# Strassen weight blocks made with single copies and single differences, and size sums added up in FP32

## The chip, the cores and the metric

One core of one Trainium2 chip runs the kernel in one launch. The metric is the device time in microseconds, from the start to the end of the launch. The engines are PE (TensorE), DVE (VectorE), ACT (ScalarE), POOL (GpSimd) and SP (SyncE, which here only issues DMAs). Each works through its own queue in order, and they wait for each other on semaphores.

## The reference

Two kinds of layer alternate, A, B, A, B, over 2048 tokens of width 1024; each adds its result to x, and both use the same weights in either round.

```
A: h = layernorm(x);  q, k, v = h @ wqkv          (32 heads of 32)
   each token attends to 8 positions: itself and 2, 4, .. 14 back
   x = x + (softmax(q.k / sqrt(32)) . v) @ wo
B: h = layernorm(x)
   x = x + (silu(h @ w1) * (h @ w3)) @ w2          (hidden width 3584)
```

## The kernel before

**Stages.** Tokens go in chunks of 512. The first A layer's q, k and v come first (to about 190 us). Then come eight units, each a B layer of one chunk: units 0 to 3 for the first round, 4 to 7 for the second. In units 1 to 4 the q, k and v of the second A layer's chunks are made behind the B layer. Attention is VectorE work: products of q and shifted k (L597), folded by a tree of additions (L510, L512, L514), a gather on PE into the PSUM tile `L` (L611), softmax, and the same tree for v (L682). The result oT goes through wo on PE (`po`, L788) and is added to x (L793). The hidden width is done in two splits, of 16 and 12 blocks of 128.

**Plain units and Strassen units.** Units 0 and 1 (`u < TU`) use plain products: `pg` (L1307) and `pu` (L1316) for w1 and w3, and `acc` (L1338) for w2. From unit 2 on (`pipeline`, `products`, tile `st`, L1074, and `w`, L1193) a product of 2 x 2 quarters is made with seven products P1 to P7 instead of eight. For that the weights are needed in FP16 as seven blocks: the four quarters and three sums and differences of them. Units 0 and 1 make these blocks beside their own work and store them to DRAM (`t_d` for w1 and w3, `t2_d` for w2); later units load them as `early`, `late` and `t2`.

**Making the blocks.** This is what the change touches. For each of 14 weight tiles (7 column groups of w1 and of w3):

- ACT squares the tile and sums it by rows (`weight_size`, L895). PE adds the 128 rows up with a product by a tile of ones (`size`, L909), DVE reduces that (L901) and makes a power of two of it (L883 to L887), `up_scale`, so that the FP16 blocks keep in range. For w2 as a whole `total_scale` does the same once (L1016).
- ACT copies the quarters, scaled, into a block buffer (`weight_sums`, L927); DVE makes the other three (`diff_steps`, L939 to L941); POOL stores the seven (L949, L950). A tile has two such blocks of columns, `a` = 0 and 1, and there are two block buffers, both in the tile `big`. A buffer is written again when its store has landed.
- For w2 (`sums_of_w2`) 14 blocks are made in the same way, with the copies at L1032 and the store at L1040.

That makes 28 blocks of w1 and w3, and 14 of w2. The two buffers, and the two PSUM banks of the pool `side`, from which `size`, `po` and `L` all take their tiles, are shared. Six other PSUM banks serve all wide products.

**Weights.** All weight tiles, the Strassen blocks too, rotate through six buffers (`wp`) in the order of the list `seq`, loaded by SP. In units 0 and 1 a buffer of w1 or w3 is given back only when its blocks are made (`release_held`), one of w2 likewise (`finish_sums`). SP issues in program order, so a load that waits holds up all that stands behind it, the DMA transposes of the normalised x (`xnT`, L272) among them, as these hold up loads.

**What sets the order.** The order of every queue is fixed when the program is built, by a planner that keeps an expected time for each engine (`now`). Each background step is yielded with its expected cost and the time from which it is ready:

```
yield 1.20, max(got["at"], stored[a]), lambda: nc.scalar.activation(...)
```

For ACT `act_background` emits steps as long as the step ends before `now["pe"] + gate[0]`, that is 2.2 us past PE's expected time. For DVE `background` takes, among the queues of makes, norms, adds, values and scores, the step that can start first and ends in time. A load, a `po` tile or a release is emitted when the planner sees its input done. So a step of another cost moves other steps too. In Strassen units the exponential of the scores (L639) is not emitted at once but put into `later` and issued by `run_later` (L1097), behind the copy of the third product of a group (P6).

Of the kernel before, what the change touches and what calls it, by code (L numbers as in the profile page):

```python
# [7 lines left out]
FP32 = mybir.dt.float32  # L8
BF16 = mybir.dt.bfloat16
FP16 = mybir.dt.float16  # L10
I32 = mybir.dt.int32
ALU = mybir.AluOpType
ACTF = mybir.ActivationFunctionType
# [4 lines left out]
def kernel(  # L18
# [13 lines left out]
    nc = tc.nc  # L32
    cfg = dict(cfg or {})
    P = 128
    _, S, D = A_x.shape
    F = B_w1.shape[1]
    KT = D // P
    W, DIL, Dh = 8, 2, 32
    assert D == 1024 and KT == 8 and D // Dh == 32
    CH = 512  # L40
# [15 lines left out]
    fsplits = [(0, 16), (16, NF)] if NF > 16 else [(0, NF)]  # L56
# [11 lines left out]
    const = ctx.enter_context(tc.tile_pool(name="const", bufs=1))  # L68
# [135 lines left out]
    HT = TCH  # L204
    big = const.tile([P, 7168], FP16, name="big")
    sums = big[:, 0:3072].rearrange("p (s k t) -> p s k t", s=3, k=KT // 2)
# [2 lines left out]
    tight = big[:, 6144:7168].bitcast(BF16).rearrange("p (i a t) -> p i a t", i=2, a=2)  # L209
    blocks = [big[:, 3584 * i:3584 * (i + 1)].rearrange("p (b k c) -> p b k c", b=7, k=KT // 2) for i in range(2)]  # L210
    NG = NF // FG
    ones = const.tile([P, P], BF16, name="ones")
    nc.gpsimd.memset(ones[:], 1.0)
    size = const.tile([P, 2, NG, 2], FP32, name="size")
    up_scale = const.tile([P, 2, NG], FP32, name="up_scale")
# [69 lines left out]
    def norm_sums(key):  # L285
# [5 lines left out]
        for name, i, out, x, y, op in (("P5", 0, s1, a21, a22, ALU.add), ("P6", 1, s2, s1, a11, ALU.subtract),  # L291
                                       ("P3", 2, s4, a12, s2, ALU.subtract), ("P7", 3, a21, a11, a21, ALU.subtract)):
            while (sums_free[i] is None) if i < 3 else key in plain_left:
# [401 lines left out]
    seq = [("qkv", which, h) for which in range(3) for h in range(2)]  # L695
    for u in range(len(units)):
        for f0, f1 in fsplits:
            if u >= TU:
                groups = [(m, g0 // FG) for g0 in range(f0, f1, FG) for m in range(2)]
                for i, (m, g) in enumerate(groups):  # L700
                    seq += [("early", m, g)] + ([("late", *groups[i - 1])] if i else [])
                seq += [("late", *groups[-1])]
            for g0 in range(f0, f1, FG) if u < TU else ():
                seq += [(kind, g0, min(FG, f1 - g0), (u, g0 // FG) if m == u else None)
                        for m, kind in enumerate(("w1", "w3"))]
            nq = (f1 - f0) // 2
            if u >= TU:
                seq += [("t2", fsplits.index((f0, f1)), b, nq) for b in (0, 2, 1, 3, 4, 6, 5)]
            else:
                seq += [("w2", g0, nq, hh) for hh in range(2) for g0 in (f0, f0 + nq)]  # L710
        if 1 <= u and u + 3 < len(units):
            seq += [("qkv", which, h) for which in range(3) for h in range(2)]
# [176 lines left out]
    def weight_size(m, g, w, at, got):  # L889

        w_ = w[:].rearrange("p k c -> p (k c)")
        half = w_.shape[1] // 2
        up, down = up_scale[:, m, g:g + 1], down_scale[:, m, g:g + 1]
        for i in range(2):
            yield 1.95, at, lambda: nc.scalar.activation(junk, w_[:, i * half:(i + 1) * half], ACTF.Square,  # L895
                                                         accum_out=size[:, m, g, i:i + 1])

        def scale_item(ps, r):
            def emit():
                opened[0] -= 1  # L900
                nc.vector.tensor_reduce(down, ps[:], op=ALU.add, axis=AX.X)  # L901
                scale_of(down, up, down)
                got["at"] = now["dve"] + 0.1
            yield 1.0, r, emit

        def add_up(t):
            ps = side_tile([P, 2], FP32, name="size", tag="sd")
            opened[0] += 1
            nc.tensor.matmul(ps[:], lhsT=ones[:], rhs=size[:, m, g, :].bitcast(BF16)[:, 1::2], start=True, stop=True)  # L909
            makes.insert(0, [scale_item(ps, pe(1, t)), None])  # L910

        t = now["act"] + 2.5
        pe_queue.append((lambda: t, lambda: add_up(t)))

    def weight_sums(m, g, w, got):

        while "at" not in got:
            yield "blocked"
        KQ = KT // 2
        for a in range(2):  # L920
            while pending[a]:
                yield "blocked"
            pending[a] += 1
            b = blocks[a]
            for i, j, fh in ((0, 2, 0), (3, 6, 1)):
                c0 = fh * 256 + a * P
                yield 1.20, max(got["at"], stored[a]), lambda: nc.scalar.activation(  # L927
                    b[:, i:j + 1:j - i], w[:, :, c0:c0 + P].rearrange("p (h k) c -> p h k c", h=2), ACTF.Copy,
                    scale=up_scale[:, m, g:g + 1])
            makes.append([differences(m, g, a, now["act"] + 0.1), None])  # L930
        made.add((m, g))

    pending, stored, made, held = [0] * 2, [0.0] * 2, set(), []
    junk = hsum[:].bitcast(BF16).rearrange("p k t -> p (k t)")

    def diff_steps(b):

        tt = nc.vector.tensor_tensor
        yield 0.66, lambda: tt(b[:, 1:5:3], b[:, 3:7:3], b[:, 0:4:3], op=ALU.subtract)  # L939
        yield 0.42, lambda: tt(b[:, 3], b[:, 4], b[:, 0], op=ALU.add)  # L940
        yield 0.42, lambda: tt(b[:, 5], b[:, 2], b[:, 3], op=ALU.subtract)  # L941

    def differences(m, g, a, r):

        b = blocks[a]
        for step in diff_steps(b):
            yield step[0], r, step[1]
        pending[a] -= 1
        nc.gpsimd.dma_start(t_d[m][g][:, 4 * a:4 * (a + 1)], b[:, 0:4])  # L949
        nc.gpsimd.dma_start(t_d[m][g][:, 8 + 3 * a:8 + 3 * (a + 1)], b[:, 4:7])  # L950
        stored[a] = now["dve"] + 7.0
# [49 lines left out]
    def total_scale(sizes_, up, down, got):  # L1001

        n = sizes_.shape[1]

        def scale_item(ps, r):
            def emit():
                opened[0] -= 1
                nc.vector.tensor_reduce(total[:], ps[:], op=ALU.add, axis=AX.X)
                scale_of(total[:], up[:], down[:])
                got["at"] = now["dve"] + 0.1  # L1010
            yield 1.1, r, emit

        def add_up(t):
            ps = side_tile([P, n], FP32, name="size", tag="sd")
            opened[0] += 1
            nc.tensor.matmul(ps[:], lhsT=ones[:], rhs=sizes_[:].bitcast(BF16)[:, 1::2], start=True, stop=True)  # L1016
            makes.insert(0, [scale_item(ps, pe(1, t)), None])

        t = now["act"] + 2.5
        pe_queue.append((lambda: t, lambda: add_up(t)))  # L1020
# [3 lines left out]
    def sums_of_w2(i, f, ws, loaded):  # L1024

        while "at" not in got2 or all(pending):
            yield "blocked"
        a = min((i for i in range(2) if not pending[i]), key=lambda i: stored[i])
        pending[a] += 1
        b = big[:, a * 3584:(a + 1) * 3584].rearrange("p (b c) -> p b c", b=7)  # L1030
        for j, (fh, hh) in ((0, (0, 0)), (3, (0, 1)), (2, (1, 0)), (6, (1, 1))):
            yield 0.61, max(loaded, stored[a], got2["at"]), lambda: nc.scalar.activation(b[:, j], ws[hh][fh][:, f, :], ACTF.Copy,  # L1032
                                                                             scale=up2[:])
        r = now["act"] + 0.1

        def rest():
            for step in diff_steps(b):
                yield step[0], r, step[1]
            pending[a] -= 1
            nc.gpsimd.dma_start(t2_d[i][:, :, f, :], b)  # L1040
            stored[a] = now["dve"] + 7.0

        makes.append([rest(), None])
        made.add(("w2", i, f))
# [12 lines left out]
    def pipeline(key, groups, consume, done, last, fill=None):  # L1057

        xnT = xnTs[key]
        KQ = KT // 2  # L1060
        sides = dict(P1=(0, xnT[:, 0:KQ, 0:HT]), P5=(1, sums[:, 0]), P6=(3, sums[:, 1]), P2=(2, xnT[:, KQ:KT, 0:HT]),
                     P7=(0, xnT[:, 0:KQ, HT:CH]), P3=(2, sums[:, 2]), P4=(1, xnT[:, KQ:KT, HT:CH]))

        def acc():
            return psum.tile([P, 2, HT], FP32, name="st", tag="mm")
# [1 line left out]
        def run(G, name, out, start, ready=0.0):  # L1067
            if name in ("P5", "P6", "P7", "P3"):
                force(adds, lambda: (key, name) in sums_at)
# [8 lines left out]
        def head_part(i, name):  # L1078
# [22 lines left out]
            elif name == "P2":  # L1101
                r = run(G, name, G["B"], False, G["tB"])
                release(1)
                consume(G, 0, G["B"][:], r)
            elif name == "P7":
                G["late"] = weight("late")
# [19 lines left out]
        for i in range(n + 1):  # L1126
            if i == n:
                staged[0] = False
                while later:
                    later.pop(0)[1]()  # L1130
            for name, tail in (("P1", "P7"), ("P5", "P3"), ("P6", "P4"), ("P2", None)):
                if i < n:
# [15 lines left out]
    def products(u, f0, f1, hold):  # L1148
# [8 lines left out]
        H11, H12, H21, H22 = [h16[:, k0:k0 + nq, t0:t0 + HT] for t0 in (0, HT) for k0 in (0, nq)]  # L1157
        left = dict(P1=H11, P2=H12, P5=hsum, P6=H11, P7=H21, P3=H12, P4=H22)
        H, ready_at, pieces, w2 = [{}, {}], {}, [0], {}
# [281 lines left out]
```

## Time and the profile before

| | |
|---|---|
| median of 3 runs | 1553.25 us (1551.62 to 1554.37) |
| profiled execution: time | 1551.62 us |
| its span, first to last instruction | 1549.7 us |
| PE, DVE, ACT, POOL busy | 1525.7, 1198.2, 874.1, 162.5 us |
| mean granted TensorE clock | 0.997 |
| size products (L909, L1016) | 15, from 194.5 to 484.1 us |
| copies of w1 and w3 quarters (L927) | 56 of 128x1024, 61.8 us busy |
| copies of w2 quarters (L1032) | 56 of 128x512, 35.5 us busy |
| differences (L939, L940, L941) | 42 each, 28.8, 17.7, 17.8 us busy |

Times in views are microseconds from the start of the span. A row of the timeline gives start, length, engine, line, operation, output and inputs, and in brackets the idle time of the engine before it and what ended that. A row of the groups gives one line's instructions of one shape: how many, their busy time in all, the mean of one in ns, and the idle time before them with its causes. A PE product overlaps the next one, so its own length (379 ns for 512 columns) is more than its share of the stream. SPq rows show the time for which SP was busy issuing.

### The profile page before, as it was taken

The numbers are of one execution on the slowest core, as the hardware profiler recorded it, in microseconds if no ns is written. First come the engines' busy times: TensorE is split into PE (matmuls) and PEld (weight loads), VectorE is DVE, ScalarE is ACT, GpSimd is POOL, SyncE is SP. The second block draws the span as 40 slices with busy tenths as digits, with TensorE's granted clock in tenths as the row PEclk, the third lists the DMA queues.
The fourth block names the chain that finished last, engine by engine and source line by source line (L and its number), as shares of the span: only waits on it lengthen the run. The fifth ranks groups of instructions, "written<-read, shape, count | busy, mean of one in ns | idle before, by whom it ended". The sixth has DMA issues, their size and how long they took to land.

```text
span 1549.7 us, 24962 instructions
## 1 busy us (share of the span) xinstructions
PE 1525.7 (98%) x9619; PEld 986.9 (64%) x9619; DVE 1198.2 (77%) x2084; ACT 874.1 (56%) x1332; POOL 162.5 (10%) x308
## 2 busy tenths in 40 slices
PE   9999999999999899999999999999999999999999
PEld 7666644444444467675685857767677667686866
DVE  4788999789869787979898967798768977445345
ACT  4885465556456246655565654655658356554634
POOL 1210111121211100102101020010102001000000
PEclk9999999999999999999999999999999999999999
DMA  9876969798687997988979888798979988878885
GB/s 331 200 225 203 275 206 298 266 319 297 215 309 268 252 322 257 332 287 298 294 257 326 317 291 282 268 325 288 325 264 310 333 305 285 295 274 339 310 294 206
DMA packets 261431, 439.55 MB, mean 284 GB/s; under 512 B 73856, under 2 KB 201088, under 8 KB 245056
## 3 DMA queue, kind: packets, MB, share of 16 engines
q1 hardware_dynamic: 248464, 390.90, 76.2%
q0 software_dynamic: 12704, 46.93, 8.4%
q8 instruction: 75, 1.23, 0.3%
q14 instruction: 44, 0.36, 0.1%
q10 hardware_dynamic: 144, 0.13, 0.0%
HBM read 345.90 MB, written 67.90 MB: 267 GB/s over the span
## 4 chain that ended last, share of the span: by engine, by line
PE 53%; DVE 11%; DMA 5%; ACT 4%; issue 2%; POOL 0%; ACTq 0%; DVEq 0%; SPq 0%; POOLq 0%
PE st L1074 27%; PE w L1193 15%; PE ps L853 7%; PE po L788 5%; DMA t_d<-big 3%; DVE tree L682 2%; DVE tree L510 2%; DVE tree L597 1%; DMA xnT<-xn 1%; DMA w3t<-in_B_w_dram 1%; DVE tree L512 1%; ACT sg L1255 1%; DMA kT<-qkv_d 1%; DVE hT L1320 1%; DVE big L939 1%
## 5 line engine op out<-in xcount | busy, mean ns | idle before, releaser
L853 PE MATMUL ps<-xnT,wqkv 128*128 128x512 f16 (+1 forms) x1472 | 322.3, 381 | 5.2 <-DMA wqkv<-in_A_wqkv_dram 3.8
L1074 PEld LDWEIGHTS <-early 128*128 128x128 f16 x2688 | 262.6, 98 | 40.7 <-issue 3.7
L853 PEld LDWEIGHTS <-wqkv 128*128 128x128 bf16 x1472 | 210.6, 144 | 115.2 <-DMA wqkv<-in_A_wqkv_dram 6.2
L1193 PE MATMUL w<-t,hT 128*128 128x512 f16 x1008 | 225.9, 379 | 1.2 <-ACT big L1213 1.1
L1074 PEld LDWEIGHTS <-late 128*128 128x128 f16 x2016 | 197.1, 98 | 31.9 <-issue 4.2
L597 DVE TENSOR_TENSOR tree<-qT,kT 128x2048 bf16<-128x2048 bf16 x128 | 156.2, 1220 | 31.2 <-ACT big L857 15.0
L510 DVE TENSOR_TENSOR tree<-tree 128x1024 bf16<-128x1024 bf16 x256 | 174.8, 683 | 0.9
L1074 PE MATMUL st<-xnT,late 128*128 128x256 f16 x1344 | 174.2, 273 | 0.7 <-DVE big L1111 0.2
L1074 PE MATMUL st<-big,early 128*128 128x256 f16 x1344 | 172.2, 273 | 1.9 <-ACT st L1086 1.8
L1193 PEld LDWEIGHTS <-hT 128*128 128x128 f16 x1008 | 98.3, 98 | 113.7 <-issue 2.4
L1074 PE MATMUL st<-xnT,early 128*128 128x256 f16 x1344 | 166.0, 273 | 0.0
L682 DVE TENSOR_TENSOR tree<-At,vT 128x2048 bf16<-128x2048 bf16 x128 | 156.0, 1219 | 11.0 <-DMA At<-E 9.6
L788 PE MATMUL po<-wo,oT 128*128 128x512 bf16 x512 | 117.7, 382 | 5.2 <-DVE down_scale L901 4.4
L1086 ACT COPY st<-st 128x512 f32<-128x512 f32 x84 | 48.4, 577 | 129.9 <-PE st L1074 129.3
L1316 PE MATMUL pu<-xnT,w3t 128*128 128x512 f16 x448 | 107.2, 383 | 2.8 <-DMA w3t<-in_B_w_dram 2.8
L857 ACT CAST hT<-ps 128x512 bf16<-128x512 f32 x96 | 55.5, 586 | 90.1 <-PE ps L853 89.0
L1307 PE MATMUL pg<-xnT,w1t 128*128 128x512 f16 x448 | 106.1, 380 | 0.0
L1338 PE MATMUL acc<-w2t,hT 128*128 128x512 bf16 x448 | 98.0, 379 | 0.2 <-DVE hT L1320 0.2
L1099 DVE TENSOR_TENSOR st<-st,big 128x512 f32<-128x512 f32 x84 | 58.4, 695 | 50.7 <-ACT big L1095 50.5
L1255 ACT ACTIVATE sg<-st,down_scale 128x512 bf16<-128x512 f32 x126 | 86.7, 688 | 12.7 <-PE st L1074 12.3
L788 PEld LDWEIGHTS <-oT 128*128 128x128 bf16 x512 | 50.1, 98 | 62.4 <-issue 8.3
L1074 PE MATMUL st<-big,late 128*128 128x256 f16 x672 | 87.1, 273 | 1.8 <-DVE st L1099 1.8
(168 smaller groups left out, 1903.1 us busy)
## 6 DMA issues: line engine op xcount, KB each, us to landing
early<-t_d SPq DMA_DIRECT2D x84, 1024.0 KB, 6.1
late<-t_d SPq DMA_DIRECT2D x84, 768.0 KB, 6.5
t<-t_d SPq DMA_DIRECT2D x42, 1024.0 KB, 7.2
t<-t_d SPq DMA_DIRECT2D x42, 768.0 KB, 5.3
wqkv<-in_A_wqkv_dram SPq DMA_DIRECT2D x28, 1024.0 KB, 7.4
w1t<-in_B_w_dram SPq DMA_DIRECT2D x14, 1024.0 KB, 8.4
w3t<-in_B_w_dram SPq DMA_DIRECT2D x14, 1024.0 KB, 11.4
t_d<-big POOLq DMA_DIRECT2D x28, 512.0 KB, 6.5
```

What stands on the lines that cost most here:

```text
L510: nc.vector.tensor_tensor(b, b, buf[:, 4:8, :], op=ALU.add)
L597: V.tensor_tensor(pr, qT[:], kT[:, :, k0:k0 + TCH], op=ALU.mult)
L682: V.tensor_tensor(tm.rearrange("p w (a e) -> p w a e", a=4), At[:].rearrange("p a w e -> p w a e"), win, op=ALU.mult)
L788: nc.tensor.matmul(ps[:], lhsT=oT[:, t, j * P:(j + 1) * P], rhs=wo[:, t, hh * 512:(hh + 1) * 512], start=(t == 0), stop=(t == KT - 1))
L853: nc.tensor.matmul(ps[:], lhsT=ws[kk // KH][:, kk % KH, t::KT], rhs=xnT[:, kk, :], start=(kk == 0), stop=(kk == KT - 1))
L1074: nc.tensor.matmul(out[:, a, :], lhsT=w[:, a, blk, k, :], rhs=rhs[:, k, :], start=start and a == 0 and k == 0, stop=k == KQ - 1, skip_grou ...
L1099: nc.vector.tensor_tensor(G["D"][:], G["D"][:], su, op=ALU.add)
L1193: nc.tensor.matmul(out[:], lhsT=lhs[:, k, j * P:(j + 1) * P], rhs=w[:, k, :], start=start and k == 0, stop=k == nq - 1, skip_group_check=True)
L1255: nc.scalar.activation(sg[:], src, ACTF.Silu, scale=inv)
L1307: nc.tensor.matmul(pg[:], lhsT=w1t[:, kk, fi * P:(fi + 1) * P], rhs=xnT[:, kk, :], start=(kk == 0), stop=(kk == KT - 1))
L1316: nc.tensor.matmul(pu[:], lhsT=w3t[:, kk, fi * P:(fi + 1) * P], rhs=xnT[:, kk, :], start=(kk == 0), stop=(kk == KT - 1))
L1338: nc.tensor.matmul(acc[:], lhsT=hT[:, f, j * P:(j + 1) * P], rhs=tiles[hh][f // nq][:, f % nq, :], start=(f == 0), stop=(f == f1 - f0 - 1))
```

## The change

The change came with the name "in Strassen units the exponential of the scores is issued on ScalarE right behind the copy of a group's third product, not as soon as its input is ready". The diff does not touch that place: `later`, `run_later` and the line that calls it stand in both programs. It does this:

- The tile of ones becomes FP32, and the size products take the FP32 sums whole, where before they took the upper 16 bits of each as BF16.
- For w1 and w3 each block's quarters are copied one by one (four ACT copies of 128x512, planned at 0.61 us) and not in pairs (two of 128x1024, planned at 1.20).
- The three derived blocks are made with four differences of 128x512 (planned at 0.40 us each) and not with one of 128x1024 and two of 128x512 (0.66, 0.42, 0.42), for w1 and w3 and for w2.
- The blocks stand at other places of the seven, and the tables that name them (`sides`, the t2 entries of `seq`) follow.

```
-    ones = const.tile([P, P], BF16, name="ones")
+    ones = const.tile([P, P], FP32, name="ones")
...
-                seq += [("t2", fsplits.index((f0, f1)), b, nq) for b in (0, 2, 1, 3, 4, 6, 5)]
+                seq += [("t2", fsplits.index((f0, f1)), b, nq) for b in range(7)]
...
-            nc.tensor.matmul(ps[:], lhsT=ones[:], rhs=size[:, m, g, :].bitcast(BF16)[:, 1::2], start=True, stop=True)
+            nc.tensor.matmul(ps[:], lhsT=ones[:], rhs=size[:, m, g, :], start=True, stop=True)
...
-            for i, j, fh in ((0, 2, 0), (3, 6, 1)):
+            for i, (kh, fh) in ((0, (0, 0)), (1, (0, 1)), (3, (1, 0)), (5, (1, 1))):
                 c0 = fh * 256 + a * P
-                yield 1.20, max(got["at"], stored[a]), lambda: nc.scalar.activation(
-                    b[:, i:j + 1:j - i], w[:, :, c0:c0 + P].rearrange("p (h k) c -> p h k c", h=2), ACTF.Copy,
+                yield 0.61, max(got["at"], stored[a]), lambda: nc.scalar.activation(
+                    b[:, i], w[:, kh * KQ:(kh + 1) * KQ, c0:c0 + P], ACTF.Copy,
                     scale=up_scale[:, m, g:g + 1])
...
-    def diff_steps(b):
-
-        tt = nc.vector.tensor_tensor
-        yield 0.66, lambda: tt(b[:, 1:5:3], b[:, 3:7:3], b[:, 0:4:3], op=ALU.subtract)
-        yield 0.42, lambda: tt(b[:, 3], b[:, 4], b[:, 0], op=ALU.add)
-        yield 0.42, lambda: tt(b[:, 5], b[:, 2], b[:, 3], op=ALU.subtract)
-
     def differences(m, g, a, r):
 
         b = blocks[a]
-        for step in diff_steps(b):
-            yield step[0], r, step[1]
+        for out, x, y in ((4, 5, 1), (1, 1, 0), (2, 4, 0), (6, 3, 2)):
+            yield 0.40, r, lambda: nc.vector.tensor_tensor(
+                b[:, out], b[:, x], b[:, y], op=ALU.add if (x, y) == (4, 0) else ALU.subtract)
...
-            nc.tensor.matmul(ps[:], lhsT=ones[:], rhs=sizes_[:].bitcast(BF16)[:, 1::2], start=True, stop=True)
+            nc.tensor.matmul(ps[:], lhsT=ones[:], rhs=sizes_[:], start=True, stop=True)
...
-        for j, (fh, hh) in ((0, (0, 0)), (3, (0, 1)), (2, (1, 0)), (6, (1, 1))):
+        for j, (fh, hh) in ((0, (0, 0)), (2, (0, 1)), (1, (1, 0)), (5, (1, 1))):
...
-            for step in diff_steps(b):
-                yield step[0], r, step[1]
+            for out, x, y in ((4, 5, 2), (2, 2, 0), (3, 4, 0), (6, 1, 3)):
+                yield 0.40, r, lambda: nc.vector.tensor_tensor(
+                b[:, out], b[:, x], b[:, y], op=ALU.add if (x, y) == (4, 0) else ALU.subtract)
...
-        sides = dict(P1=(0, xnT[:, 0:KQ, 0:HT]), P5=(1, sums[:, 0]), P6=(3, sums[:, 1]), P2=(2, xnT[:, KQ:KT, 0:HT]),
-                     P7=(0, xnT[:, 0:KQ, HT:CH]), P3=(2, sums[:, 2]), P4=(1, xnT[:, KQ:KT, HT:CH]))
+        sides = dict(P1=(0, xnT[:, 0:KQ, 0:HT]), P5=(1, sums[:, 0]), P6=(2, sums[:, 1]), P2=(3, xnT[:, KQ:KT, 0:HT]),
+                     P7=(0, xnT[:, 0:KQ, HT:CH]), P3=(1, sums[:, 2]), P4=(2, xnT[:, KQ:KT, HT:CH]))
```

## The prediction

> **What bounds the kernel now.** I read the page's first part first, then the busy times of four stretches.
>
> ```profile
> span 1549.7 us, 24962 instructions
> PE 1525.7 (98%) x9619; PEld 986.9 (64%) x9619; DVE 1198.2 (77%) x2084; ACT 874.1 (56%) x1332; POOL 162.5 (10%) x308
> ```
>
> ```profile
> 0.00:194.00 194.00, 192.51 (x1105) 126.49 (x1106) 148.74 (x244) 118.99 (x196) 26.74 (x62) 1.00 0.84 247
> 194.00:524.00 330.00, 321.46 (x1500) 143.74 (x1497) 285.80 (x560) 189.44 (x233) 57.55 (x94) 0.99 0.82 269
> 524.00:620.00 96.00, 88.82 (x576) 63.62 (x577) 68.38 (x114) 44.12 (x71) 4.36 (x8) 0.98 0.89 287
> 620.00:1550.00 930.00, 922.94 (x6443) 653.09 (x6440) 695.26 (x1168) 521.60 (x834) 73.90 (x144) 1.00 0.86 296
> ```
>
> The columns after the length are PE, PEld, DVE, ACT and POOL busy, then granted clock, DMA share and GB/s. PE bounds every stretch. The edited work all lies from 194 to 524 us (the size products run from 194.5 to 484.1 us), and just there and behind it PE loses time: 8.5 and 7.2 us idle, at a granted clock of 0.99 and 0.98. Past 620 us it idles 7 us in 930, so what is won or lost before reaches the end. Where PE stands still, its timeline says (start, length, idle before and what ended it):
>
> ```profile
> 286.90 6.80 PE L788 MATMUL po<-wo,oT 128*128 128x512 bf16 x24 [2.65 <-DVE down_scale L901]
> 387.40 1.89 PE L788 MATMUL po<-wo,oT 128*128 128x512 bf16 x8 [1.44 <-DVE down_scale L901]
> 467.05 3.31 PE L1316 MATMUL pu<-xnT,w3t 128*128 128x512 f16 x8 [2.79 <-DMA w3t<-in_B_w_dram]
> 507.18 15.70 PE L1338 MATMUL acc<-w2t,hT 128*128 128x512 bf16 x72
> 524.30 1.08 PE L853 MATMUL ps<-xnT,wqkv 128*128 128x512 f16 x4 [1.43 <-DVE peak L1051]
> 529.18 6.00 PE L853 MATMUL ps<-xnT,wqkv 128*128 128x512 f16 x20 [3.79 <-DMA wqkv<-in_A_wqkv_dram]
> ```
>
> A wide product takes 0.216 us here (72 in 15.70). The eight behind the stall at 467.05 take 3.31: after a gap of 2.6 us or more PE runs at half speed for a while, after 1.44 us it does not. Why wqkv is late, the SP queue's timeline shows:
>
> ```profile
> 488.80 0.95 SPq L547 DMA_DIRECT2D vT<-qkv_d  x1
> 510.68 4.34 SPq L272 DMA_TRANSPOSE xnT<-xn  x2
> 515.07 2.29 SPq L724 DMA_DIRECT2D wqkv<-in_A_wqkv_dram  x2
> 518.78 10.14 SPq L272 DMA_TRANSPOSE xnT<-xn  x2
> ```
>
> SP stands still from 489.8 to 510.7: a transpose waits for DVE's xn (20.9 us), and two weight loads wait behind it.
>
> **The removed and added work.** These groups price it (last columns: busy, mean ns):
>
> ```profile
> L927 ACT ACTIVATE big<-w3t,up_scale 128x1024 f16<-128x1024 bf16 x28 | 31.1, 1141 | 19.2 <-DMA t_d<-big 15.5 <-DVE up_scale L887 3.7
> L939 DVE TENSOR_TENSOR big<-big 128x1024 f16<-128x1024 f16 x42 | 28.8, 686 | 20.2 <-ACT big L927 10.7 <-ACT big L1032 9.5
> L940 DVE TENSOR_TENSOR big<-big 128x512 f16<-128x512 f16 x42 | 17.7, 422 | 1.0
> L909 PE MATMUL size<-size,ones 128*128 128x2 bf16 x14 | 2.3, 167 | 0.0
> L909 PEld LDWEIGHTS <-ones 128*128 128x128 bf16 x14 | 1.4, 98 | 1.7
> 517.11 2.56 ACT L1032 ACTIVATE big<-w2t,up 128x512 f16<-128x512 bf16 x4 [7.62 <-DMA t_d<-big]
> ```
>
> ACT: each of the 28 w1 and w3 blocks gets four 128x512 copies for two 128x1024 ones. Four such copies take 2.56 us on end, two wide ones 2.17 (236.45 us), so +0.39 x 28 = +10.9 us. The 14 w2 blocks keep their four. DVE: each of 42 blocks gets four differences (4 x 0.422) for 0.686 + 0.422 + 0.424, so +0.16 x 42 = +6.7 us. I take both at nothing for the end: PE's own work hides them. ACT is busy 189 of 330 us and waits 68 us for PE's pg there; DVE is busy 286 and waits 20 us for ACT, 17 for PE. Without that cover the larger would count, 10.9 us. POOL's stores stand 0.16 us later each. The block numbers and the load order of the seven t2 parts change names only: P1, P2, P5, P6, P7, P3, P4 are loaded in the same order and size. The FP32 memset of ones is at the start, where nothing waits for it.
>
> PE: the 15 size products get FP32 operands. A BF16 one now costs about 0.03 us (the next product starts 0.03 behind it, at 282.34 and 282.37), as the load of ones hides under the product before. No FP32 product is in this trace. From below: 0.03 as now. From above: two strided loads (0.144, L853) and two wide products (0.386, L611), 1.06 us. I take twice the row it is nearest to, as the operands have twice the bytes: 2 x (0.098 + 0.167) = 0.53, 0.50 more than now, x 15 = **+7.5 us** (0 to 15.5), all on PE and all before 484 us.
>
> The Trainium skill speaks against this edit: "FP8 and Floating Point Precision", TensorE Precision Notes, says that true FP32 takes four passes through the array. With four times 0.265 us each product would cost 1.06 and the edit 15.5 us, and my sum would end at +1.4 us.
>
> **What moves.** The program is laid out by a planner that fits ACT and DVE steps into gaps that it expects, so the steps' new sizes (0.61 for 1.20 us, 0.40 for 0.66 and 0.42) reorder the queues. I compared the two programs' orders, counted in PE products. PE's order is the same up to the first size product and again over its last 11,961 products; all between is rearranged. Step by step:
>
> (a) wqkv. The first two loads come 15.6 us of products earlier, ahead of the four transposes instead of behind two, since their weight blocks are finished sooner. Between the end of acc (522.87) and full speed (532.19) PE does 11 products, 2.4 us of work in 9.3: **-6.9 us**. Next late would be the k weights behind the transposes, wanted 13.8 us after.
> (b) The stall at 286.9. The second po tile needs the PSUM buffer of the size product, and DVE's reduce of it (L901) stood behind a difference (L939) that waited for an ACT copy. In the new order po comes 10.4 us after that size product, so the reduce is done. 2.65 us, and 7 products at 0.42 us until 289.84: **-4.1 us**. DVE's own wait stays, hidden by three pairs of PSUM buffers, 3 x 3.46 us of products.
> (c) The same pattern at 387.4: no po stands right behind that size product any more, **-1.4 us**.
> (d) The w3t stall. SP waited 18.4 us for the w2 copies that free its buffer. In the new order these copies stand 8.7 us earlier and the load 10.2 us. 2.79 us, and 9 products at 0.43 us: **-4.7 us**.
>
> A rule of "TensorE: Matmul & The Clock Gate" (What's actually happening) puts the fall to half clock at about 3.4 us of idling. Here gaps of 2.65 and 2.79 us were enough; by the rule (b) and (d) would be worth 2.7 and 2.8 us, and the sum would end 3.3 us higher.
>
> (e) New waits. A new order brings its own. Of the weight loads that now have under 20 us of products between the freeing of their buffer and their first use, all in the stretch gain time but two (the k weights, 4 us less); past it four of unit 2 lose 3 to 5 us. I take **+3 us**, between 0 and the 17.1 that go.
>
> **The sum.** -6.9 - 4.1 - 1.4 - 4.7 + 7.5 + 3.0 = -6.6 us. The profiled execution took 1551.62 us (span 1549.7, 1.9 around it), giving 1545.0; the median of the runs, 1553.25, is 1.63 above it: **1546.6 us**. About 0.2%, 3.1 us, is what a measurement of this kernel can tell from no change.
>
> **The rivals.** *The waits come back (slower).* Two block buffers carry all 42 blocks, and a copy waits until the store of the buffer's last block has landed; ACT already waits 42.5 us for that, 7.6 at the longest. The new order asks for copies up to 9 us sooner, but the stores land no sooner, so ACT may sit longer in front of a Silu. Past 10.4 us, the three pairs of PSUM buffers, PE stops. If this gives back the 17.1 us, the sum is 7.5 + 0: 1560.8 us. For it: the copies are split finer, but the store cycle is the same. Against: all of today's waits are under the bound.
>
> *The FP32 product is dear.* At the upper price of 1.06 us the sum is -17.1 + 15.5 + 3 = +1.4: 1554.7 us, within no change.
>
> *Nothing happens to the end.* The change is named after the exponential of the scores, but no line of the diff touches that: the exponential already waits in both programs for the copy of the third product, and past unit 2 ACT's order is the same. If the rearranged waits equal the old ones and the products hide: 1553 us.
>
> **How the numbers follow.** Forecast 0.52 (its own range 1537 to 1550), waits come back 0.31, dear product 0.12 (0.10 of it within 0.2%), nothing 0.05. So faster 0.52, same 0.15, slower 0.33. Low end 1537: all stalls gone, the product at its low price (1536.2) left just outside. High end 1563: the first rival with 2 us to spare; the dear product on top of it (1568.8) is left out.
>
> **What would show it.** The FP32 size products' own rows settle the price: 0.5 us in PE's order each. A PE timeline with no gap at 282 to 290, 460 to 470 and 520 to 530 us, and two wqkv loads on SP before the transposes, show (a) to (d) right. ACT rows with t_d waits above 10 us and PE gaps behind them show the first rival. I am wrong in the main if PE's idle time from 194 to 620 us is not below the 15.7 us of now.

## The result and the profile after

The changed kernel takes 1530.45 us (median of 4 runs, 1530.20 to 1530.72), beside 1552.43 us (1550.77 to 1554.37) for the kernel before on the same chip: a ratio of 0.9858, 95% interval 0.9841 to 0.9875. That is 22 us faster. The prediction said 1546.6 us, 1537 to 1563: the direction was right, the size was not, and the time lies below the range.

The page's first part, of the profile after:

```profile
span 1528.5 us, 25134 instructions
PE 1519.7 (99%) x9634; PEld 989.3 (65%) x9634; DVE 1202.3 (79%) x2126; ACT 884.7 (58%) x1388; POOL 160.0 (10%) x308
```

The busy times by stretch, cut as they were for before (length, then PE, PEld, DVE, ACT, POOL busy, granted clock, DMA share, GB/s):

```profile
194.00:524.00 330.00, 330.00 (x1566) 153.78 (x1565) 292.81 (x609) 202.51 (x294) 56.56 (x94) 1.00 0.86 281
524.00:620.00 96.00, 96.00 (x677) 70.99 (x676) 87.37 (x144) 55.06 (x88) 7.14 (x15) 1.00 0.90 314
```

PE's idle time from 194 to 620 us was 15.7 us and is now none, at full clock. ACT and DVE have 10.6 and 4.1 us more to do than before, and nobody waits for that.

PE's timeline of after at the first and the last of the places where before stood still. No row from 194 to 608 us has an idle time in brackets:

```profile
282.23 0.28 PE L909 MATMUL size<-size,ones 128*128 128x2 f32 x2
282.37 1.89 PE L1302 MATMUL pg<-xnT,w1t 128*128 128x512 f16 x8
...
292.72 3.62 PE L788 MATMUL po<-wo,oT 128*128 128x512 bf16 x16
...
502.46 10.52 PE L1333 MATMUL acc<-w2t,hT 128*128 128x512 bf16 x48
512.82 17.43 PE L853 MATMUL ps<-xnT,wqkv 128*128 128x512 f16 x80
```

The po tiles come 10.4 us behind the size product, and 80 products of wqkv follow the end of acc without a break. SP's timeline of after:

```profile
484.79 0.52 SPq L547 DMA_DIRECT2D vT<-qkv_d  x1
485.41 4.14 SPq L724 DMA_DIRECT2D wqkv<-in_A_wqkv_dram  x2
504.63 12.04 SPq L272 DMA_TRANSPOSE xnT<-xn  x4
516.77 2.85 SPq L724 DMA_DIRECT2D wqkv<-in_A_wqkv_dram  x4
```

The two weight loads now leave before SP waits for the transposes' xn, not behind that. ACT's copies, in the groups of after from 194 to 620 us:

```profile
L1026 ACT ACTIVATE big<-w2t,up 128x512 f16<-128x512 bf16 x56 | 36.3, 711 | 42.5 <-DMA t_d<-big 34.9 <-DVE x_sb L1347 3.9 <-DVE big L1032 1.8
L927 ACT ACTIVATE big<-w1t,up_scale 128x512 f16<-128x512 bf16 x56 | 36.1, 711 | 6.0 <-DMA t_d<-big 6.0
```

ACT waits 34.9 + 6.0 us for block stores, at most 6.3 us at once, under the 10.4 us from which PE would stand.

**Where the time came from.** The same PE instructions, by their starts in the two traces:

| place in PE's order | before | after | gained since the row above | forecast |
|---|---|---|---|---|
| first size product of L909 | 205.12 | 205.07 | 0.05 | 0 |
| end of unit 1's acc | 522.88 | 512.98 | 9.85 | -0.3 |
| first st of unit 2 | 571.98 | 554.96 | 7.12 | 6.9 |
| the st that waits 0.41 us for ACT in both | 695.85 | 674.95 | 3.88 | 0 |
| end of the span | 1549.7 | 1528.5 | 0.3 | 0 |

The forecast of -0.3 is (b), (c) and (d) less the FP32 products and (e): 10.2 - 7.5 - 3.0. An "end" is the end of the row, start and length added.

### The profile page after: what moved, and what is told of

The parts are those of the page before. It is cut to its first block, busy times and chain, and to the rows that moved or that the text cites. A ratio compares the mean times of both kernels' runs of the same rounds, so it can differ in the third digit from the quotient of the medians.

```text
span 1528.5 us, 25134 instructions
## 1 busy us (share of the span) xinstructions
PE 1519.7 (99%) x9634; PEld 989.3 (65%) x9634; DVE 1202.3 (79%) x2126; ACT 884.7 (58%) x1388; POOL 160.0 (10%) x308
## 4 chain that ended last, share of the span: by engine, by line
PE 94%; ACT 3%; DVE 2%; issue 1%; DMA 0%; SPq 0%; ACTq 0%; DVEq 0%
PE st L1069 31%; PE ps L853 21%; PE w L1188 15%; PE po L788 7%; PE pg L1302 6%; PE acc L1333 6%; PE pu L1311 6%; PE pq L444 1%; ACT sg L1250 1%; PE L L611 0%; ACT L639 0%; DMA wqkv<-in_A_wqkv_dram 0%; DVE hT L1159 0%; DVE tree L597 0%; ACT L1250 0%
## 5 line engine op out<-in xcount | busy, mean ns | idle before, releaser
L1250 ACT ACTIVATE sg<-st,down_scale 128x512 bf16<-128x512 f32 x126 | 86.7, 688 | 11.9 <-PE st L1069 11.6
```

Source lines behind the costliest of these rows:

```text
L1250: nc.scalar.activation(sg[:], src, ACTF.Silu, scale=inv)
```

## The experiments

My theory after the result: the instructions themselves hardly matter. The planned sizes of the steps rearrange the queues, and the new order lacks the waits of the old one. Its rivals: smaller ACT and DVE instructions let urgent work through sooner; and, inside the theory, finer steps are better by nature, or the order of before merely had accidents. "Before" is timed beside each; its median was 1549.8 to 1550.6 us.

### Order or instructions: each kernel in the other's order

**e7_before_fine_plan**, the old instructions in the new order:

```
-                yield 1.20, max(got["at"], stored[a]), lambda: nc.scalar.activation(
+                yield 0.61, max(got["at"], stored[a]), lambda: None
+                yield 0.61, max(got["at"], stored[a]), lambda: nc.scalar.activation(
...
-        yield 0.66, lambda: tt(b[:, 1:5:3], b[:, 3:7:3], b[:, 0:4:3], op=ALU.subtract)
-        yield 0.42, lambda: tt(b[:, 3], b[:, 4], b[:, 0], op=ALU.add)
-        yield 0.42, lambda: tt(b[:, 5], b[:, 2], b[:, 3], op=ALU.subtract)
+        yield 0.40, lambda: tt(b[:, 1:5:3], b[:, 3:7:3], b[:, 0:4:3], op=ALU.subtract)
+        yield 0.40, lambda: None
+        yield 0.40, lambda: tt(b[:, 3], b[:, 4], b[:, 0], op=ALU.add)
+        yield 0.40, lambda: tt(b[:, 5], b[:, 2], b[:, 3], op=ALU.subtract)
```

> The kernel before with its own instructions (paired copies, the paired difference, BF16 size products), but planned in the steps of the changed kernel: each paired copy is yielded as an empty step and a step of 0.61 us, the differences as 0.40, 0.40 (empty), 0.40, 0.40. The products of PE and the DMAs of SP then stand in the order of the changed kernel. Theory (the sizes of the planned steps rearrange the queues, and the order alone takes the waits away): as fast as the changed kernel or up to 2 us faster, 1528 to 1531 us, since it keeps the cheaper BF16 size products. Rival (the smaller instructions themselves do it: a copy or difference of half the size lets an urgent step through sooner): no better than halfway, 1540 us or more.

**e8_after_coarse_plan**, the new instructions in the old order (of w1 and w3; w2 likewise):

```
-            for i, (kh, fh) in ((0, (0, 0)), (1, (0, 1)), (3, (1, 0)), (5, (1, 1))):
-                c0 = fh * 256 + a * P
-                yield 0.61, max(got["at"], stored[a]), lambda: nc.scalar.activation(
...
+            for pair in (((0, 0, 0), (3, 1, 0)), ((1, 0, 1), (5, 1, 1))):
+                yield 1.20, max(got["at"], stored[a]), lambda: [nc.scalar.activation(
...
+        for cost, some in ((0.66, ((4, 5, 1), (1, 1, 0))), (0.42, ((2, 4, 0),)), (0.42, ((6, 3, 2),))):
```

> The changed kernel with its own instructions (single copies, single differences, FP32 size products), but planned in the steps of the kernel before: two copies to a step of 1.20 us, two differences to a step of 0.66. The products of PE and the DMAs of SP then stand in the order of the kernel before. Theory (order alone): the waits of before come back, with 1.6 us for the FP32 products and the later end of the copies on top: 1552 to 1557 us. Rival (the smaller instructions themselves): near the changed kernel, under 1540 us.

Measured: e7 1531.19 us, ratio 0.9875 (0.9861 to 0.9890); e8 1555.32 us, ratio 1.0038 (1.0028 to 1.0049). In the traces the products of PE and the DMAs of SP and POOL stand in one order in e7 and the changed kernel, and in one order in e8 and before. With all its old instructions the kernel is as fast as the changed one; with all the new ones in the old order it is slower than before. PE's timeline of e8 has the old stalls, each at most 2.3 us from where it was:

```profile
287.83 5.34 PE L788 MATMUL po<-wo,oT 128*128 128x512 bf16 x24 [2.94 <-DVE down_scale L901]
388.91 3.32 PE L788 MATMUL po<-wo,oT 128*128 128x512 bf16 x8 [3.03 <-DVE down_scale L901]
...
531.16 15.12 PE L853 MATMUL ps<-xnT,wqkv 128*128 128x512 f16 x60 [3.87 <-DMA wqkv<-in_A_wqkv_dram]
582.27 1.03 PE L1068 MATMUL st<-big,late 128*128 128x256 f16 x8 [1.55 <-DVE st L1093]
```

So the order makes the gain, and the new instructions by themselves, in the old order, cost 0.3 to 0.5%. That settles the main question. The last row is the wait that before has at 580 us and that my sum left out. The order alone does not make that one: e7, in the new order, waits 1.53 us at the same place (561.97 us).

### The FP32 size products

**e1_before_fp32** is before with the FP32 products alone; **e2_after_bf16** is the changed kernel without them; **after_again** is the changed kernel once more, as their yardstick. The edit, which e2 takes back:

```
-    ones = const.tile([P, P], BF16, name="ones")
+    ones = const.tile([P, P], FP32, name="ones")
...
-            nc.tensor.matmul(ps[:], lhsT=ones[:], rhs=size[:, m, g, :].bitcast(BF16)[:, 1::2], start=True, stop=True)
+            nc.tensor.matmul(ps[:], lhsT=ones[:], rhs=size[:, m, g, :], start=True, stop=True)
```

> The kernel before with the FP32 tile of ones and the FP32 sums of the size products, and nothing else; the order of every queue is that of before. The prediction's term (0.53 us a product, 0.50 more than in BF16, fifteen times): +7.5 us. The page's four passes: +15.5 us. Theory from the trace of the changed kernel (the next product starts 0.14 us behind an FP32 one, 0.11 more than in BF16): +1.6 us.

> The changed kernel with the BF16 size products of before; the order of every queue is that of the changed kernel. The prediction's term: 7.5 us faster than the changed kernel. Theory: 1.6 us faster, and so the fastest of all versions if nothing else moves; the planned order, not the FP32 sums, makes the gain.

> The changed kernel itself, timed beside the others, so that versions a few tenths of a per cent apart are told from it on the same chip: 1529 to 1531 us.

**e9_after_fp32_x8** issues each FP32 size product eight times:

```
-            nc.tensor.matmul(ps[:], lhsT=ones[:], rhs=size[:, m, g, :], start=True, stop=True)
+            for _ in range(8):
+                nc.tensor.matmul(ps[:], lhsT=ones[:], rhs=size[:, m, g, :], start=True, stop=True)
```

(and the same for the one of w2)

> The changed kernel with each of the fifteen FP32 size products issued eight times over, on the same operands into the same tile, so that the price of one stands out: 105 products more. Prediction's price of 0.53 us: +56 us. The page's four passes, 1.06 us: +111 us. Theory, 0.14 us: +15 us, all of it on PE, between 194 and 485 us.

Measured: e1 1551.96 us, ratio 1.0009 (1.0000 to 1.0018), so 0 to 2.8 us slower, and not 7.5. e2 1530.91 us beside 1530.83 for after_again: no difference. e9 1554.60 us, 23.8 us over after_again for 105 products: 0.226 us each, more than the 0.14 that I expected and well under 0.53. (0.60 us of the 23.8 is a wait for DVE's st at 585.61 us; without it 0.22 each.)

The rows of the size product's line in after say what one is (least, median and longest duration in ns, first and last start):

```profile
L909 PEld LDWEIGHTS size<-size,ones x28: 190/190/190, 204.9 to 474.7; 128*128 128x128 f32 x28
L909 PE MATMUL size<-size,ones x28: 167/210/251, 205.1 to 474.7; 128*128 128x2 f32 x28
```

There are fourteen such products, so each runs as two weight loads of 190 ns and two matmuls. "FP8 and Floating Point Precision" of the Trainium skill (TensorE Precision Notes) speaks of four passes; these rows show two, and the measurement decides. What a single one costs the stream is in PE's timeline of after further up (282.23 and 282.37). Eight on end, in PE's timeline of e9:

```profile
206.96 1.84 PE L910 MATMUL size<-size,ones 128*128 128x2 f32 x16
208.66 0.59 PE L1304 MATMUL pg<-xnT,w1t 128*128 128x512 f16 x2
```

Alone, the next product starts 0.14 us later. Eight take 1.70, so each further one takes (1.70 - 0.14) / 7 = 0.22 us. A single product is cheaper than a further one. The likely reason, read from the rows and not tried: of its two loads the first runs beside the wide product ahead (204.9 us, before the start at 205.07), and a further product has no wide one ahead. My expectation for e9 took the price of the single one for all.

Why does e2 gain nothing? Its first st of unit 2 starts at 553.88 us, 1.38 before that of after_again (555.26). Then its timeline shows a wait that the changed kernel does not have:

```profile
561.13 1.03 PE L1069 MATMUL st<-big,late 128*128 128x256 f16 x8 [0.97 <-DVE st L1094]
```

DVE adds that st at 560.38 us in e2, at 560.73 in after_again and at 560.03 in after. PE came 1.4 us sooner than in after_again, DVE only 0.35: behind the old stalls DVE is the next to be late, and it takes most of what PE wins ahead of it. e7, with BF16 products too, waits 1.53 us at the same place.

### One part at a time

**e3_before_single_copies** has the single copies alone, **e4_before_single_diffs** the single differences alone:

```
-            for i, j, fh in ((0, 2, 0), (3, 6, 1)):
+            for i, (kh, fh) in ((0, (0, 0)), (2, (1, 0)), (3, (0, 1)), (6, (1, 1))):
...
-                yield 1.20, max(got["at"], stored[a]), lambda: nc.scalar.activation(
+                yield 0.61, max(got["at"], stored[a]), lambda: nc.scalar.activation(
```

> The kernel before with the quarters of w1 and w3 copied one by one (four ACT copies planned at 0.61 us for two at 1.20) and nothing else: the paired difference and the BF16 size products stay. In its order the first two wqkv loads of unit 2 stand ahead of the transposes, with 29 and 25 us of products between the freeing of their buffers and their first use. Theory (finer steps let the planner put the making of the blocks, and all behind it, earlier; either part is enough for (a)): 1530 to 1540 us. Rival (it takes both parts, or the differences): 1548 us or more.

```
-        yield 0.66, lambda: tt(b[:, 1:5:3], b[:, 3:7:3], b[:, 0:4:3], op=ALU.subtract)
-        yield 0.42, lambda: tt(b[:, 3], b[:, 4], b[:, 0], op=ALU.add)
-        yield 0.42, lambda: tt(b[:, 5], b[:, 2], b[:, 3], op=ALU.subtract)
+        yield 0.40, lambda: tt(b[:, 4], b[:, 6], b[:, 3], op=ALU.subtract)
+        yield 0.40, lambda: tt(b[:, 1], b[:, 3], b[:, 0], op=ALU.subtract)
+        yield 0.40, lambda: tt(b[:, 3], b[:, 4], b[:, 0], op=ALU.add)
+        yield 0.40, lambda: tt(b[:, 5], b[:, 2], b[:, 3], op=ALU.subtract)
```

> The kernel before with four single differences, planned at 0.40 us each, and nothing else: the paired copies and the BF16 size products stay. In its order the first two wqkv loads of unit 2 stand ahead of the transposes too, with 22 and 18 us of products before their first use. Theory (either part is enough for (a)): 1530 to 1540 us, and the two parts do not add up, as both together gave 20 to 22 us. Rival (the copies do it, since ACT's steps are those that became finer by half): 1548 us or more.

Measured: e3 1529.69 us, ratio 0.9870 (0.9855 to 0.9885); e4 1531.61 us, ratio 0.9882 (0.9865 to 0.9899). Either part alone brings the whole gain, though e3 touches only ACT's steps and e4 only DVE's, and e4's steps add up to more planned time than before (1.60 us for 1.50). The longest PE wait of e3 from 194 to 620 us is 0.35 us; e3 has the lowest median of all, but its interval covers that of the changed kernel.

### Finer steps, or another order?

Two numbers of the plan alone, both made coarser, with all instructions as before:

**e10_before_copies_130:**

```
-                yield 1.20, max(got["at"], stored[a]), lambda: nc.scalar.activation(
+                yield 1.30, max(got["at"], stored[a]), lambda: nc.scalar.activation(
```

> The kernel before with one number changed: a paired copy is planned at 1.30 us in place of 1.20, so its instructions are the same and its steps coarser still. In its order the two wqkv loads stand ahead of the transposes, and no po tile stands right behind the size product at 280.8 us of products; the pair of po tiles at 379 and 386 stays behind its size product, as in the kernel before. Theory A (finer steps are what wins): no gain, 1548 us or more. Theory B (the order of before has accidents that nearly any other order lacks): (a) and (b) go, (c) stays with its 1.4 us: 1531 to 1540 us.

**e11_before_diffs_076:**

```
-        yield 0.66, lambda: tt(b[:, 1:5:3], b[:, 3:7:3], b[:, 0:4:3], op=ALU.subtract)
+        yield 0.76, lambda: tt(b[:, 1:5:3], b[:, 3:7:3], b[:, 0:4:3], op=ALU.subtract)
```

> The kernel before with one number changed: the paired difference is planned at 0.76 us in place of 0.66, which makes the three steps 1.60 us together, as long as the four of 0.40 in the changed kernel. In its order the two wqkv loads stand ahead of the transposes and no po tile stands right behind a size product. Theory A (finer steps): no gain, 1548 us or more. Theory B (accidents of one order): 1530 to 1536 us.

Measured: e11 1531.96 us, ratio 0.9880 (0.9864 to 0.9897); e10 1541.16 us, ratio 0.9939 (0.9924 to 0.9954). A tenth of a microsecond on one planned cost, with no instruction changed, is worth as much as the whole change within the intervals. So finer steps are not the cause (theory A falls). Theory B holds for e11; e10 lies just above its range of 1531 to 1540, as the theory named the wrong remainder. The pair of po tiles that it expected to stall costs 0.25 us there, and another accident of the old order is still in place, (d). PE's timeline of e10:

```profile
463.62 3.60 PE L1316 MATMUL pu<-xnT,w3t 128*128 128x512 f16 x8 [4.58 <-DVE tree L510]
467.00 2.90 PE L1307 MATMUL pg<-xnT,w1t 128*128 128x512 f16 x8
469.74 1.89 PE L1316 MATMUL pu<-xnT,w3t 128*128 128x512 f16 x8
```

The releaser named in the first row, a step of the tree on DVE, frees nothing that `pu` needs. ACT's timeline names what came at that moment, and SP's timeline says when it was sent for:

```profile
463.59 1.91 ACT L895 ACTIVATE hsum<-w3t 128x2048 bf16<-128x2048 bf16 x1 [2.19 <-DMA w3t<-in_B_w_dram]
```

```profile
450.20 0.38 SPq L744 DMA_DIRECT2D w3t<-in_B_w_dram  x1
```

The load was issued at 450.20 us and landed 13.4 later. In after the same load is issued at 438.26 us, 11.9 earlier, and PE does not wait. The stall in e10 costs 4.58 us and, with 16 products in 6.12 us in place of 3.46 at half speed, 2.66 more: 7.2 us. Then DVE is late, and PE is slow again behind that wait:

```profile
570.55 1.05 PE L1074 MATMUL st<-big,late 128*128 128x256 f16 x8 [2.27 <-DVE st L1099]
571.42 1.89 PE L1074 MATMUL st<-big,early 128*128 128x256 f16 x8
573.10 1.90 PE L1074 MATMUL st<-xnT,late 128*128 128x256 f16 x8
```

The wait is 2.27 us, and the 16 products from 571.42 to 574.81 take 1.6 us more than at full speed. Together that makes 11.1 us; the profiled execution of e10 (span 1540.5 us) is 11.6 longer than that of after_again (1528.9).

### One stall at a time: the place of the wqkv loads

**e5_after_late_wqkv** puts the stall (a) back into the changed kernel (in `flush`, the two loads wait for two transposes); **e6_before_early_wqkv** takes it alone out of the kernel before (two transposes are kept until the two loads are issued):

```
         while due:
+            if len(w_tiles) in (50, 51) and len(turned) < 29:
+                break
```

> The changed kernel with the first two wqkv loads of unit 2 held until two of the four transposes in front of them are issued, as in the kernel before; nothing else moves before 500 us. Theory (step (a) of the prediction: the place of these loads on SP is worth 6.9 us, as the spans between the same products say 7.2): 1535 to 1538 us, with a gap of PE behind the end of acc. Rival (the wait was the end of a chain that the earlier rearrangement had already shortened, so that the transposes are no longer late): under 1532 us.

```
+            if key == ("B", 0, 2) and len(w_tiles) < 52:
+                behind.append(turn)
+            else:
+                turn()
...
+        while len(w_tiles) == 52 and behind:
+            behind.pop(0)()
```

> The kernel before with the first two wqkv loads of unit 2 put ahead of the two transposes that stood before them; PE's order is unchanged. Theory (step (a), which adds up with the others): 1545 to 1547 us, 6.9 faster than before, if the loads find their buffers free, which in this order are given back later than in the changed kernel; the gap at 529.18 us goes. Rival (what is late is not the place on SP but the buffer: the loads then wait for the blocks made from the tile): 1551 to 1553 us, with the same gap.

Measured: e5 1541.14 us, ratio 0.9939 (0.9925 to 0.9954), some 10 us slower than the changed kernel where I expected 7; e6 1545.90 us, ratio 0.9977 (0.9967 to 0.9987), 3.9 us faster than before where I expected 6.9. PE's timeline of e5:

```profile
516.68 1.93 PE L855 MATMUL ps<-xnT,wqkv 128*128 128x512 f16 x4 [3.41 <-DMA wqkv<-in_A_wqkv_dram]
522.09 16.73 PE L855 MATMUL ps<-xnT,wqkv 128*128 128x512 f16 x68 [3.49 <-DMA wqkv<-in_A_wqkv_dram]
```

and of e6:

```profile
506.38 15.70 PE L1345 MATMUL acc<-w2t,hT 128*128 128x512 bf16 x72
564.25 1.04 PE L1081 MATMUL st<-xnT,early 128*128 128x256 f16 x8
...
573.55 1.03 PE L1081 MATMUL st<-big,late 128*128 128x256 f16 x8 [3.03 <-DVE st L1106]
574.42 1.84 PE L1081 MATMUL st<-big,early 128*128 128x256 f16 x8
```

In e6 the way from the end of acc (506.38 + 15.70 = 522.08) to the first st of unit 2 (564.25) takes 42.2 us. It took 49.1 before and takes 42.0 in after. So (a) is worth 6.9 us, as forecast, and by its place on SP alone. But then PE stands before DVE's st for 3.03 us, where it was 1.76 before, and the eight products at 574.42 run at half speed: 2.5 us of the 7.7 that e6 is ahead at the first st are given back by 583.95 us. In e5 the same way, with the same 200 products, takes 52.0 us (513.27 to 565.26), 10.0 more than in after. (Behind 528 us the planner lays e5 out in another order, so what follows the first st is not compared.) The upstream stalls are gone there, PE reaches the end of acc 9.6 us sooner than before, and DVE's xn does not come as much sooner: SP gets past its first transposes' wait 8.3 us ahead of that end and not 12.2. The same stall costs more when PE is less late. The pieces of this gain do not add up; each is bounded by what is late next.

## Why the prediction was right and wrong

- **What bounds and where: right.** PE's idle time between 194 and 620 us was what the change could win, and all 15.7 us of it went, with the half speed behind it. ACT's and DVE's extra work was rightly taken at nothing: e7 has none of it and is no faster. One figure is misread: in the traces the two programs share the order of the last 5,980 of some 9,600 PE products, from 685.7 us of before on; 11,961 is about twice that, products and weight loads together.
- **(a) -6.9: right.** 7.1 us between the same instructions, and e6 shows the same 6.9 alone.
- **(b), (c), (d), -10.2 together: right.** The end of acc came 9.85 us sooner. That is 10.2, less the FP32 products' 1.4 us, plus two waits of 0.33 and 0.22 us that I did not list (at 214.30 and 497.45 us); 0.5 us is left over. e8 brings (b) and (c) back by the order alone, and e10, where (d) remains, pays 7.2 us for it. The half speed in (b) and (d) was read rightly from before, but the rule drawn from it (a gap of 2.6 us or more) does not hold in the runs (last section): in e8 the gap of (b) is 2.94 us and PE goes on at full speed. How a stall of the old order splits is not fixed: in e1, e6 and e8 the w3t wait is 0.7 to 0.9 us, and the next wait, acc for hT, is 1.9 to 2.2 us.
- **FP32 products +7.5: the term mis-sized most.** I doubled the BF16 pair of load and matmul because the operands have twice the bytes, and took it to stand on PE in full. It delays PE by 0.09 to 0.11 us a product, 1.4 to 1.6 us in all, near the low bound and a fifth of what I took; and in the changed kernel nearly nothing of that reaches the end, as e2 shows. The estimate of 15.5 us from the four passes of "FP8 and Floating Point Precision" would have been wrong by ten times.
- **(e) new waits +3: wrong.** There were none: PE stands for no load from 194 us on. I had put a price on a doubt that no row carried.
- **Unit 2 at 0: wrong.** The waits at 580.01, 602.96 and 614.86 us (1.76, 0.78, 0.41) stood in the stretch from 524 to 620 us that I had shown with its 7.2 us idle, and I priced only what belonged to wqkv. They went too, 3.88 us with the short gaps around them. All three stand in e8 again, with the old order (1.55, 0.78, 0.41), but only the second comes and goes with the order: it is in e1, e6 and e8, which have PE's old order, and in no other run. The first is a close race with DVE in either order, 0 in the changed kernel, 0.97 in e2, 1.53 in e7 and 3.03 in e6. The third is in e5 and e10 too. So part of the 3.9 us could not have been read from the order alone.
- **The sum:** 6.1 (FP32) + 3.0 (e) + 3.9 (unit 2) + 1.1 (end of acc) + 0.2 (a) + 0.3 (the rest) = 14.6 us, which is the span's 21.2 less the forecast 6.6. The range's low end failed for the same reason: it let go only the stalls on my list.
- **Rivals.** "The waits come back" did not happen: no store wait past 6.3 us. "FP32 product is dear" fell with e1. "Nothing happens to the end" was right that the exponential is untouched, and wrong that the waits would equal the old ones.

## What to carry to other kernels

Where a planner fixes the queues, a changed planned cost is a change of all orders downstream: first compare the orders, then price every wait of the old order that the new one lacks, the whole stretch long, before costing the instructions. Planning the old instructions with the new costs separates the two in a single run. One order among several may be unlucky: here a tenth of a microsecond on one planned cost, and no other edit, brought 18 us, so it pays to try a few planned costs before rewriting anything.

## What was not expected of the hardware

- An FP32 product of 128x128 by 2 columns ran as two weight loads of 190 ns and two matmuls: 0.14 us to the next product when it stands alone, 0.22 each on end.
- PE fell to half speed behind gaps of 2.27 us (e10, at 570.55 us), 2.54 (e1, at 287.22), 2.65 (before and e6), 2.79 (before) and 3.03 (e6 and e8), but not behind one of 2.94 us (e8 at 287.83: 24 products in 5.34 us), nor behind one of 2.24 (e6 at 496.66). So the length of the gap alone does not decide. All of these gaps are below the idle window of about 3.4 us in "TensorE: Matmul & The Clock Gate", What's actually happening.
- What does decide can be read from the granted clock; it was not tried by an experiment, but all 14 traces fit. From 190 us to the end of the work the clock falls and recovers only at ticks 3.41 us apart, whenever PE's gaps begin: in before it falls to 0.50 at 286.48, 467.38 and 528.83 us, 53 and 18 ticks from one another. It fell wherever PE had been idle for 2.2 us or more of the 3.41 before a tick (2.23 in before up to 286.48, 2.27 in e10 up to 571.43), and nowhere after 1.8 us or less; between 1.8 and 2.2 there is no case. The gap of 2.94 us in e8 lay across a tick, 1.14 us before 286.03 and 1.80 behind it, and cost no clock; the one of 2.24 in e6 was split into 1.57 and 0.67. The clock stays down for at least one tick, and for two or three where PE stood idle again (6.83 us in e1, 10.24 in e5). So a stall of 2.3 to 3 us cost 1.4 to 1.9 us more here, or nothing more, by where it fell on the ticks.
